# Two maxima over the partitions: from a GpSimd reduction to small matmuls and VectorE

## The chip, the cores and the metric

The kernel runs on one core of a Trainium2 chip. The metric is the device time of one execution in microseconds (us); where several executions of one kernel stand together, their median is given. Five engines work side by side, each through its own instructions in program order: PE (TensorE, matrix products; its weight loads are shown as PEld), DVE (VectorE), ACT (ScalarE), POOL (GpSimd) and SP (SyncE, which here issues every DMA).

## The reference

Input `x` has 8192 positions of 448 channels. The first half filters along the positions, the second is a gated feed-forward net. `mod` is six rows of 448, computed from a condition vector.

```python
    h = _layernorm(x, axis=-1) * (1 + ca) + sa
    x = x + ga * _A_ref(h, A_w1, A_b1, A_w2, A_b2)   # rfft, 2-layer complex block MLP, soft threshold, irfft
    h = _layernorm(x, axis=-1) * (1 + cb) + sb
    x = x + gb * _B_ref(h, B_w_gate, B_w_up, B_w_down)
    # _B_ref: (gelu(h @ w_gate) * (h @ w_up)) @ w_down, with F = 1792
```

Nothing in the reference asks for a maximum over partitions. The kernel needs two, because it carries fp32 factors as a pair of 16-bit halves and picks a power of two as the scale of each matrix: one maximum bounds the norms of the columns of `w_gate` and `w_up`, the other the rows of `w_down`.

## The kernel before, in words

There are three stages. The first (0 to 95 us) takes statistics of `x` and does the first part of the Fourier transform. The second (95 us, its first `ps`, to about 420 us) does its second part, the block MLP, the soft threshold and the first part of the inverse, and in its shadow it loads the feed-forward weights, finds their scales and splits them. The third (its matmuls on L985 run from 441.5 to 1994 us) is the last part of the inverse and the feed-forward net.

The change lies in the second stage. Its work is cut into 32 units `(h, bt)`, a half of the channels and a block of four frequencies. A loop `step(i)` works on four units at once, as a software pipeline, and the order in which it calls the parts is the order in which each engine runs them (`manual_schedule`: nothing is moved). In one step PE does, in this order:

- `stage_s2` of unit i (24 matmuls, tile `ps`); ACT and DVE split the result into `zh` and `zl`,
- `stage_m2` of unit i-2, twice (12 matmuls each, tile `pm`); DVE clips it (`t`, L427) and subtracts (`y`, four instructions on L435); `split_y` turns `y` into `yh` on ACT and `yl` on POOL,
- `stage_i1` of unit i-3, two groups of three matmuls (tile `pi`, L464 to L466); ACT copies each into `us` (L467), and SP stores `us` (`vd`, L469),
- `stage_m1` of unit i-1 (24 matmuls); ACT and DVE split it into `hh` and `hl`.

POOL's other work in a step is `tl`, the low half of the next unit's input, which PE needs for `stage_s2`.

PSUM has eight banks, used as four pairs by tag. `stage_i1` and the small products for norms take theirs from the pair `pd`. A new tile takes a bank of its pair that is free.

Side work hangs on hooks of a step, at places called `load`, `pe`, `act`, `dve`. `at(i, hook, fn)` puts `fn` there. Short DVE operations don't run at once: `later(V)` puts each into the list `tiny`, and `drip()` issues one from it. `drip()` is called eight times a step: after each `zl` (2), after each `t` and each group of `y` (4), and after each `hl` (2). So short operations stand singly between the long ones.

`row_scales` runs at step 9. At the end of step 16 `scales1` and `scales2` go into the list. They take the maximum of the norms over a partition's columns (`mx`), then over the partitions (`mxa`), and derive the scales `sw`, `dsw`, `dg`, `sa_act`, `isa`. At step 18 `down_scales` follows for `w_down` (`hs`, then `ds_d`), at step 19 `down_scales2`. The maximum over partitions is one POOL instruction, put into the same list by `GL = later(G)`. From step 18 `weights_hi` (ACT) and `weights_lo` (DVE in even steps, L709; POOL in odd ones, L711) scale and split one loaded piece `raw` per step with `sw`.

All short operations that go through `later` carry one line in the profile, L480, so they are told apart by their tiles.

Of the kernel before, what the change touches and what calls it, by code (L numbers as in the profile page):

```python
# [11 lines left out]
F32 = mybir.dt.float32  # L12
F32R = mybir.dt.float32r
F16 = mybir.dt.float16
BF16 = mybir.dt.bfloat16
I32 = mybir.dt.int32
AF = mybir.ActivationFunctionType
ALU = mybir.AluOpType

N = 8192  # L20
D = 448
# [8 lines left out]
NFT = F // 128  # L30
NP = NFT // 2
# [11 lines left out]
def spectral_geglu(ctx, tc, x, w1, b1, w2, b2, wg, wu, wd, cvec, wmod, cf1, cs2, cmi, cgm, out):  # L43
    nc = tc.nc
    V, S, G, T = nc.vector, nc.scalar, nc.gpsimd, nc.tensor
# [9 lines left out]
    cpool = ctx.enter_context(tc.tile_pool(name="cpool", bufs=1))  # L55
    psum = ctx.enter_context(tc.tile_pool(name="psum", bufs=2, space=bass.MemoryType.PSUM))

    def bank(tag, name):
        return psum.tile([128, 512], F32, tag=tag, name=name)
# [12 lines left out]
    nrm = cpool.tile([128, 2, NFT], F32, name="nrm")  # L72
# [3 lines left out]
    ds_d = cpool.tile([128, 1], F32, name="ds_d")  # L76
    sa_act = cpool.tile([128, NP], F32, name="sa_act")
    isa = cpool.tile([128, NP], F32, name="isa")
    rmax = cpool.tile([128, 2], F32, name="rmax")
# [4 lines left out]
    mpool = mctx.enter_context(tc.tile_pool(name="mpool", bufs=1, side="right"))  # L84
# [5 lines left out]
    sa0 = mpool.tile([112, NBLK], F32, name="sa0")  # L90
    mih = mpool.tile([128, 2, 128], F32R, name="mih")
    mil = mpool.tile([128, 2, 128], F32R, name="mil")

    def split(hi, lo, src, eh=None, el=None):

        (eh or S.copy)(hi, src)  # L96
        h = hi.bitcast(F32) if hi.dtype == F32R else hi
        (el or V).tensor_tensor(lo, src, h, ALU.subtract)  # L98
# [26 lines left out]
    with ExitStack() as actx:  # L125
# [136 lines left out]
        pe, start = 0.0, {}  # L262
        for g, bs in enumerate(groups):
# [5 lines left out]
            at = [pos[0] + 0.06] + [pos[i] + d for i in (1, 2, 3) for d in (0.03, 0.06)] + [pos[3] + 0.1]  # L269
            if g == 0:  # L270
                at = [t_stats[e] + 0.2] + [pos[0] + 0.03] * 7
            for t_, f in zip(at, scale_steps(bs)):
                ex(t_, f)
            for bb in bs:
                pe = start[bb] = max(pe + 0.75, at[-1] + 0.3)
# [20 lines left out]
    with ExitStack() as bctx:  # L296
# [178 lines left out]
        tiny = []  # L475
# [13 lines left out]
        VL, GL = later(V), later(G)  # L489
# [7 lines left out]
        def at(i, hook, fn, *args):  # L497
            side.setdefault((i, hook), []).append((fn, args))
# [77 lines left out]
        def inv_pow2(d, s):  # L576
            VL.tensor_scalar(d.bitcast(I32), s.bitcast(I32), -1.0, float(254 << 23), op0=ALU.mult, op1=ALU.add)
# [67 lines left out]
            ps = raws.pop(("s", pr, j))  # L645
            V.tensor_scalar(nrm[:, pr, 2 * j : 2 * j + 2], ps[:, 0:2], 1.02, 1e-30, op0=ALU.mult, op1=ALU.add)

        def all_max(dst, src):
            GL.partition_all_reduce(dst, src, 128, bass_isa.ReduceOp.max)

        mxa = cpool.tile([128, 2], F32, name="mxa")
        dsw = cpool.tile([128, 2], F32, name="dsw")
        hs = cpool.tile([128, 1], F32, name="hs")

        def scales1():

            ni = nrm.bitcast(I32)
            VL.tensor_scalar(ni, ni, 1, 0x7F800000, op0=ALU.logical_shift_right, op1=ALU.bitwise_and)
            VL.tensor_scalar(ni, ni, float(65 << 23), None, op0=ALU.add)
            mx = cpool.tile([128, 2], F32, name="mx")  # L660
            VL.tensor_reduce(mx, nrm, mybir.AxisListType.X, ALU.max)
            all_max(mxa, mx)

        def scales2():
            pow2(sw, mxa)
            inv_pow2(dsw, sw)
            inv_pow2(hs, sk)
            VL.tensor_scalar(dsw, dsw, hs, None, op0=ALU.mult)
            VL.tensor_copy(dg, dsw[:, 0:1])

            VL.tensor_tensor(hs, rmax[:, 0:1], rmax[:, 1:2], ALU.add)
            VL.tensor_tensor(hs, hs, hs, ALU.mult)
            VL.tensor_scalar(hs, hs, 1.02 * D, 1e-30, op0=ALU.mult, op1=ALU.add)
            mx2 = cpool.tile([128, NFT], F32, name="mx2")
            VL.tensor_tensor(mx2, nrm[:, 0], nrm[:, 1], ALU.mult)
            VL.tensor_scalar(mx2, mx2, hs, None, op0=ALU.mult)

            VL.tensor_tensor(sa_act, mx2[:, :NP], mx2[:, NP:], ALU.max)
            pow2(sa_act, sa_act, 13)
            inv_pow2(isa, sa_act)  # L680
            VL.tensor_scalar(sa_act, sa_act, dsw[:, 1:2], None, op0=ALU.mult)

        def down_scales():

            VL.tensor_tensor(dsc, dn[:, :NP], dn[:, NP:], ALU.max)
            VL.tensor_tensor(dsc, dsc, isa, ALU.mult)
            VL.tensor_reduce(hs, dsc, mybir.AxisListType.X, ALU.max)
            VL.tensor_scalar(hs, hs, 1e-30, None, op0=ALU.max)
            all_max(ds_d, hs)

        def down_scales2():
            pow2(hs, ds_d, 13)
# [43 lines left out]
            at(2 + 2 * j, "load", pre, npool, ("m", j), load_m, j)  # L736
            at(3 + 2 * j, "dve", down_max, j)
        at(9, "dve", row_scales)
        at(16, "dve", scales1)
        at(16, "dve", scales2)  # L740
        for i in range(1, 17):
            step(i)
        nctx.close()
# [105 lines left out]
    with ExitStack() as cctx:  # L849
# [206 lines left out]
        def down(i):  # L1056
# [59 lines left out]
        first = {  # L1116
            0: [(split_g, 1), (split_v, 1), (parts_hi, 2)],
            2: [(inverse, 1), (parts_hi, 3), (residual, 1), (parts_lo, 2, V, V)],
            3: [(sums_hi, 2), (stats2, 1)],
            4: [(rsqrt_part, 1, 5), (parts_hi, 4), (sums_lo, 2, G), (load_d8, 5), (rsqrt_part, 1, 4)],  # L1120
            5: [(parts_lo, 3, V, G), (rsqrt_part, 1, 5)],
            7: [(sums_hi, 3), (sums_lo, 3, V), (load_d8, 6)],
            8: [(norm2, 1, 0), (norm2, 1, 1), (parts_lo, 4, G, G), (parts_hi, 5)],
            10: [(pack_hi, 1), (parts_lo, 5, V, V), (pack_lo, 1), (sums_hi, 4)],
# [128 lines left out]
```

## Time and profile before

| | us |
|---|---|
| median of 3 runs | 2016.02 |
| lowest, highest | 2013.63, 2016.29 |
| the profiled execution | 2015.5 |
| its span in the profile | 2013.7 |

| busy, share of the span | PE | weight loads | DVE | ACT | POOL |
|---|---|---|---|---|---|
| whole kernel | 96% | 85% | 57% | 38% | 59% |

The span is what the profiler saw from the first to the last instruction; the profiled execution's own time is 1.8 us longer. The mean granted clock of TensorE over the span was 0.98 of full speed. A row of a timeline gives the start, the duration, the engine, the line, the operation, its tiles, and in brackets the idle time before it and what ended that. A row of the waits gives who waited for whom, the total in us, how often, and the longest. A row of a table by stretches gives for each engine its busy time, then the granted clock of TensorE, the share of the DMA engines and their rate.

### The profile page before, as it was taken

The numbers are of one execution on the slowest core, as the hardware profiler recorded it, in microseconds if no ns is written. First come the engines' busy times: TensorE is split into PE (matmuls) and PEld (weight loads), VectorE is DVE, ScalarE is ACT, GpSimd is POOL, SyncE is SP. The second block draws the span as 40 slices with busy tenths as digits, with TensorE's granted clock in tenths as the row PEclk, the third lists the DMA queues.
The fourth block names the chain that finished last, engine by engine and source line by source line (L and its number), as shares of the span: only waits on it lengthen the run. The fifth ranks groups of instructions, "written<-read, shape, count | busy, mean of one in ns | idle before, by whom it ended". The sixth has DMA issues, their size and how long they took to land.

```text
span 2013.7 us, 43598 instructions
## 1 busy us (share of the span) xinstructions
PE 1927.9 (96%) x17674; PEld 1712.5 (85%) x17674; DVE 1147.2 (57%) x2409; ACT 768.0 (38%) x1293; POOL 1197.2 (59%) x1492
## 2 busy tenths in 40 slices
PE   6799978987999999999999999999999999999999
PEld 3498968966888989898888888888888889889898
DVE  6578858868555554555555555455555555555533
ACT  3566646745233333333333333333333333333322
POOL 3444435548566666666666666666666666666644
PEclk8899988988999999999999999999999999999999
DMA  9886646741111111111111111111111111111000
GB/s 390 283 222 165 175 117 165 199 123 52 51 42 43 42 43 43 43 43 43 43 43 44 49 42 45 50 42 42 42 50 42 42 42 42 42 43 44 21 17 19
DMA packets 165569, 157.72 MB, mean 78 GB/s; under 512 B 86388, under 2 KB 146424, under 8 KB 165368
## 3 DMA queue, kind: packets, MB, share of 16 engines
q1 hardware_dynamic: 165368, 154.94, 26.6%
q8 instruction: 138, 2.26, 0.5%
q14 instruction: 63, 0.52, 0.1%
HBM read 95.09 MB, written 44.04 MB: 69 GB/s over the span
## 4 chain that ended last, share of the span: by engine, by line
PE 81%; DVE 9%; DMA 4%; ACT 2%; POOL 2%; issue 1%; SPq 1%; DVEq 0%; ACTq 0%; POOLq 0%
PE pgu L985 49%; PE pdn L1053 7%; PE pdn L1051 7%; PE pdn L1052 7%; DVE y L435 2%; DMA td<-st 2%; PE ps L183 1%; DMA raw<-in_B_w_up 1%; DVE t L427 1%; DVE zl L350 1%; DVE hl L405 1%; PE pi L885 1%; PE pi L883 1%; PE pi L884 1%; PE ps L343 1%
## 5 line engine op out<-in xcount | busy, mean ns | idle before, releaser
L985 PE MATMUL pgu<-nt,wh 128*128 128x256 f16 x6272 | 835.0, 273 | 1.2 <-DVE x L1026 1.2
L985 PEld LDWEIGHTS <-wh 128*128 128x128 f16 x6272 | 603.1, 98 | 99.3 <-issue 31.3
L985 PE MATMUL pgu<-nt,wl 128*128 128x256 f16 (+1 forms) x3584 | 502.4, 273 | 1.5 <-DVE x L1026 1.3
L1021 ACT ACTIVATE gel<-pgu,dg 128x256 f32<-128x256 f32 x448 | 200.0, 472 | 788.6 <-PE pgu L985 748.9
L1051 PE MATMUL pdn<-wd,ac 128*128 128x224 f16 x1568 | 407.8, 260 | 4.3 <-DVE x L894 2.3
L1053 PE MATMUL pdn<-wd,ac 128*128 128x224 f16 x1568 | 407.7, 260 | 0.2 <-DVE ac L1044 0.2
L1052 PE MATMUL pdn<-wd,ac 128*128 128x224 f16 x1568 | 407.7, 260 | 0.0
L1032 POOL TENSOR_TENSOR x<-x 128x128 f32<-128x128 f32 x223 | 239.9, 1076 | 234.7 <-DVE x L1026 234.7
L1044 DVE SCALAR_TENSOR_TENSOR ac<-x,sa_act,ac 128x896 f16<-128x896 f32 (+1 forms) x225 | 308.4, 1370 | 81.5 <-ACT ac L1043 81.5
L985 PEld LDWEIGHTS <-wl 128*128 128x128 f16 (+1 forms) x3584 | 298.1, 97 | 59.5 <-issue 26.1
L1026 DVE TENSOR_TENSOR x<-pgu,gel 128x256 f32<-128x256 f32 x448 | 179.6, 418 | 284.4 <-ACT gel L1021 283.7
L1043 ACT ACTIVATE ac<-x,sa_act 128x896 f16<-128x896 f32 (+1 forms) x225 | 233.0, 1035 | 53.1 <-POOL x L1035 51.2
L1086 POOL TENSOR_TENSOR o<-u,p 128x224 f32<-128x224 f32 x32 | 21.0, 656 | 292.7 <-DVE u L1085 292.7
L1033 POOL TENSOR_TENSOR x<-x 128x128 f32<-128x128 f32 x223 | 158.5, 711 | 17.5
L1052 PEld LDWEIGHTS <-ac 128*128 128x128 f16 x1568 | 154.1, 98 | 5.4 <-issue 4.7
L1051 PEld LDWEIGHTS <-ac 128*128 128x128 f16 x1568 | 154.1, 98 | 1.0 <-issue 0.2
L1053 PEld LDWEIGHTS <-ac 128*128 128x128 f16 x1568 | 154.1, 98 | 0.9 <-DVE ac L1044 0.5
L98 POOL TENSOR_TENSOR yl<-y,yh 128x448 fp32r<-128x448 f32 x63 | 74.8, 1189 | 81.1 <-ACT yh L96 81.1
L1034 POOL TENSOR_TENSOR x<-x 128x128 f32<-128x128 f32 x223 | 112.4, 504 | 0.0
L98 POOL TENSOR_TENSOR tl<-tr,th 128x896 f16<-128x896 f32 x30 | 57.7, 1924 | 89.0 <-DMA tr<-td 38.5
L1035 POOL TENSOR_TENSOR x<-x 128x128 f32<-128x128 f32 x223 | 108.1, 485 | 0.0
L435 DVE TENSOR_TENSOR y<-pm,t 64x224 f32<-64x224 f32 x256 | 99.5, 389 | 8.7 <-DVE t L427 0.5
(292 smaller groups left out, 2831.8 us busy)
## 6 DMA issues: line engine op xcount, KB each, us to landing
td<-st SPq DMA_DIRECT2D x16, 896.0 KB, 9.6
tr<-td SPq DMA_DIRECT2D x64, 224.0 KB, 4.3
vd<-us SPq DMA_DIRECT2D x64, 224.0 KB, 2.9
xx<-in_A_x SPq DMA_DIRECT2D x32, 448.0 KB, 3.4
v<-vd SPq DMA_DIRECT2D x64, 224.0 KB, 2.8
out<-x SPq DMA_DIRECT2D x31, 448.0 KB, 2.7
xt<-in_A_x SPq DMA_DIRECT2D x15, 896.0 KB, 17.2
nt<-pk SPq DMA_TRANSPOSE x480, 2.3
```

Of the source, the lines that this page charges most:

```text
L98: (el or V).tensor_tensor(lo, src, h, ALU.subtract)
L435: V.tensor_tensor(y[ri * 64 : ri * 64 + 64, gi], pv[si, ri], tv[si, ri], ALU.subtract)
L985: T.matmul(pgu[i, t, q][:, pr * H : (pr + 1) * H], w[rows, tw, f0 : f0 + 128], nts[i][rows, tn, :], start=start, stop=stop, skip_group_che ...
L1021: S.activation(gl, ps[:, :H], AF.Gelu_apprx_tanh, scale=dg)
L1026: V.tensor_tensor(dst, ps[:, H : 2 * H].rearrange("p (b c) -> p b c", b=2), gl.rearrange("p (b c) -> p b c", b=2), ALU.mult)
L1032: e.tensor_tensor(s1, a21, a22, ALU.add)
L1033: e.tensor_tensor(s2, s1, a11, ALU.subtract)
L1043: S.activation(ac[:, 0, k], x[:, k], AF.Copy, scale=sc)
L1044: V.scalar_tensor_tensor(ac[:, 1, k], x[:, k], sc, ac[:, 0, k], op0=ALU.mult, op1=ALU.subtract)
L1051: T.matmul(ps, ac[:, 0, ka], wds[t][:, 0, kb], start=t == 0, stop=False)
L1052: T.matmul(ps, ac[:, 0, ka], wds[t][:, 1, kb], start=False, stop=False)
L1053: T.matmul(ps, ac[:, 1, ka], wds[t][:, 0, kb], start=False, stop=t == NP - 1)
```

## The change

`all_max` no longer calls POOL. It rounds a column of n values per partition to bf16 (`mxc`), multiplies it with an identity on PE so that the 128 partitions come to lie along a row of PSUM (`turn`, tile `pmx`), reduces that row on DVE (`mxt`), puts the n results on a diagonal (`mxd`), and multiplies that with ones so that every partition receives them (`spread`), from where DVE copies them to the target. The values are powers of two, which bf16 holds exactly; for the second maximum an extra instruction clears the mantissa first. Between a result and its reader stand either three operations of other work, given as `first` and `then`, or three empty entries of the list. For the first maximum those six are operations that `scales2` had at a later place (`hb2`, `mx2`, `sa_act`). `scales1` and `scales2` move from the end of step 16 (`dve`) to its start (`pe`). A bf16 identity and a row of ones are made at the start of the kernel.

```diff
+    identb = mpool.tile([128, 128], BF16, name="identb")
+    make_identity(nc, identb)
+    onesr = mpool.tile([2, 128], BF16, name="onesr")
+    V.memset(onesr, 1.0)
...
-        def all_max(dst, src):
-            GL.partition_all_reduce(dst, src, 128, bass_isa.ReduceOp.max)
+        def all_max(dst, src, n, first=(), then=()):
+            col = mpool.tile([128, n], BF16, name="mxc")
+            top = mpool.tile([n, 1], F32, name="mxt")
+            dia = mpool.tile([n, n], BF16, name="mxd")
+            at_ = {}
+            free = lambda: None
+            def turn():
+                at_[0] = bank("pd", "pmx")
+                T.matmul(at_[0][:n, :128], col, identb, start=True, stop=True)
+            def spread():
+                T.matmul(at_[0][:, 128 : 128 + n], onesr[:n], dia, start=True, stop=True)
+            VL.tensor_copy(col, src)
+            tiny.extend(first or [free] * 3)
+            tiny.append(turn)
+            tiny.append(lambda: V.tensor_reduce(top, at_[0][:n, :128], mybir.AxisListType.X, ALU.max))
+            VL.tensor_scalar(dia, identb[:n, :n], top, None, op0=ALU.mult)
+            tiny.extend(then or [free] * 3)
+            tiny.append(spread)
+            tiny.append(lambda: V.tensor_copy(dst, at_[0][:, 128 : 128 + n]))
...
-            all_max(mxa, mx)
+            hb2 = cpool.tile([128, 1], F32, name="hb2")
+            mx2 = cpool.tile([128, NFT], F32, name="mx2")
+            first = [
+                lambda: V.tensor_tensor(hb2, rmax[:, 0:1], rmax[:, 1:2], ALU.add),
+                lambda: V.tensor_tensor(hb2, hb2, hb2, ALU.mult),
+                lambda: V.tensor_scalar(hb2, hb2, 1.02 * D, 1e-30, op0=ALU.mult, op1=ALU.add),
+            ]
+            then = [
+                lambda: V.tensor_tensor(mx2, nrm[:, 0], nrm[:, 1], ALU.mult),
+                lambda: V.tensor_scalar(mx2, mx2, hb2, None, op0=ALU.mult),
+                lambda: V.tensor_tensor(sa_act, mx2[:, :NP], mx2[:, NP:], ALU.max),
+            ]
+            all_max(mxa, mx, 2, first, then)
...
         def scales2():
...
-            VL.tensor_tensor(hs, rmax[:, 0:1], rmax[:, 1:2], ALU.add)
-            VL.tensor_tensor(hs, hs, hs, ALU.mult)
-            VL.tensor_scalar(hs, hs, 1.02 * D, 1e-30, op0=ALU.mult, op1=ALU.add)
-            mx2 = cpool.tile([128, NFT], F32, name="mx2")
-            VL.tensor_tensor(mx2, nrm[:, 0], nrm[:, 1], ALU.mult)
-            VL.tensor_scalar(mx2, mx2, hs, None, op0=ALU.mult)
-            VL.tensor_tensor(sa_act, mx2[:, :NP], mx2[:, NP:], ALU.max)
...
         def down_scales():
...
-            all_max(ds_d, hs)
+            VL.tensor_single_scalar(hs.bitcast(I32), hs.bitcast(I32), 0x7F800000, ALU.bitwise_and)
+            all_max(ds_d, hs, 1)
...
-        at(16, "dve", scales1)
-        at(16, "dve", scales2)
+        at(16, "pe", scales1)
+        at(16, "pe", scales2)
```

The order on POOL around the first maximum, before. `tl` and `yl` are the low halves of the input and of `y`; a row ISA without tiles is not arithmetic.

```order
L98 TENSOR_TENSOR tl<-tr,th 128x896 [waits DMAHW6_49,DMAHW7_49,PE_49,Activation_49]
L98 TENSOR_TENSOR yl<-y,yh 128x448 [waits PE_49,Activation_49] x2
L480 ISA
L480 ISA mxa<-mx 128x2 [waits DVE_49]
L98 ISA
L98 TENSOR_TENSOR tl<-tr,th 128x896 [waits DMAHW2_49,DMAHW3_49,PE_49,Activation_49]
L98 TENSOR_TENSOR yl<-y,yh 128x448 [waits PE_49,Activation_49] x2
```

And after (line numbers are three higher at this place):

```order
L101 TENSOR_TENSOR tl<-tr,th 128x896 [waits DMAHW6_49,DMAHW7_49,PE_49,Activation_49]
L101 TENSOR_TENSOR yl<-y,yh 128x448 [waits PE_49,Activation_49] x2
L101 TENSOR_TENSOR tl<-tr,th 128x896 [waits DMAHW2_49,DMAHW3_49,PE_49,Activation_49]
L101 TENSOR_TENSOR yl<-y,yh 128x448 [waits PE_49,Activation_49] x2
L101 TENSOR_TENSOR tl<-tr,th 128x896 [waits DMAHW0_49,DMAHW7_49,PE_49,Activation_49]
```

The reduction and the two ISA rows around it are gone, so `tl` follows `yl` directly; at the second maximum the same three rows go.

The order on PE at `stage_i1` of step 17, before:

```order
L419 MATMUL pm2_3400<-w2h_94,hl_3312 128x224
L464 MATMUL pi1_3423<-yh_3239,mih_98 128x448 [waits PE_49]
L465 MATMUL pi1_3423<-yl_3240,mih_98 128x448 [waits Pool_49]
L466 MATMUL pi1_3423<-yh_3239,mil_99 128x448
L464 MATMUL pi1_3428<-yh_3276,mih_98 128x448 [waits PE_49]
L465 MATMUL pi1_3428<-yl_3277,mih_98 128x448 [waits Pool_49]
L466 MATMUL pi1_3428<-yh_3276,mil_99 128x448
```

And after:

```order
L422 MATMUL pm2_3418<-w2h_94,hl_3329 128x224
L665 LDWEIGHTS onesr_105
L665 MATMUL pmx_3332<-mxd_3195,onesr_105 128x2 [waits DVE_49]
L467 MATMUL pi1_3441<-yh_3256,mih_98 128x448 [waits PE_49]
L468 MATMUL pi1_3441<-yl_3257,mih_98 128x448 [waits Pool_49]
L469 MATMUL pi1_3441<-yh_3256,mil_99 128x448
L467 MATMUL pi1_3446<-yh_3295,mih_98 128x448 [waits Activation_49]
L468 MATMUL pi1_3446<-yl_3296,mih_98 128x448 [waits Pool_49]
L469 MATMUL pi1_3446<-yh_3295,mil_99 128x448
```

The `spread` product has come in ahead of the stage, and the second group of `pi` now waits for ACT: `pmx` holds one bank of the pair `pd` from step 16 until its copy late in step 17, so both groups use the other bank, and the second needs ACT's copy of the first. Step 20 has the same.

The order on DVE in steps 16 and 17 after the change, from the first reduction to the copy of its result (`y` stands for four instructions):

```order
L483 TENSOR_REDUCE mx<-nrm 128x2
L438 TENSOR_TENSOR y<-pm_3234,t 64x224 x4
L483 CAST mxc<-mx 128x2
L430 TENSOR_SCALAR t<-pm_3260 128x448
L691 TENSOR_TENSOR hb_3191<-rmax 128x1
L438 TENSOR_TENSOR y<-pm_3260,t 64x224 x4
L692 TENSOR_TENSOR hb_3191<-hb_3191 128x1
L408 SCALAR_TENSOR_TENSOR hl<-pm_3299,hh_808 112x2x256
L693 TENSOR_SCALAR hb_3191<-hb_3191 128x1
L408 SCALAR_TENSOR_TENSOR hl<-pm_3316,hh_809 112x2x256
L353 SCALAR_TENSOR_TENSOR zl<-ps_3354,ca_96,zh_804 112x2x256
L670 TENSOR_REDUCE mxt<-pmx 2x1
```

Before, these places held no short operation until the end of step 16, and `sw<-mxa`, which waits for POOL, stood three places behind `mx`; now the list runs from step 16 to step 21.

More of the change, by code (lines that the diff above doesn't have):

```diff
@@ L6 @@
 import concourse.tile as tile
-from concourse import bass_isa
 from concourse import mybir
```

## Prediction

> **What bounds the kernel now.** I read the page first, for what ends last, then the waits of the second stage, then that stage cut into stretches of 10 us, then its timeline by engine. The page's chain of work that ended last is mostly PE's:
>
> ```profile
> PE 81%; DVE 9%; DMA 4%; ACT 2%; POOL 2%; issue 1%; SPq 1%; DVEq 0%; ACTq 0%; POOLq 0%
> ```
>
> The third stage, where nearly all of PE's share lies, is not touched. What counts is the second stage, where PE should be busy too. From the stretches (busy us of PE, PEld, DVE, ACT, POOL, then the clock granted to TensorE), an undisturbed one, and three around the two maxima:
>
> ```profile
> 240.00:250.00 10.00, 10.00 (x99) 9.76 (x98) 9.00 (x19) 5.48 (x11) 4.62 (x4) 1.00 0.49 121
> 260.00:270.00 10.00, 2.37 (x23) 2.37 (x23) 4.49 (x14) 3.67 (x7) 4.05 (x3) 0.63 0.25 68
> 300.00:310.00 10.00, 0.91 (x7) 0.71 (x7) 8.54 (x19) 2.98 (x6) 3.19 (x3) 0.51 0.17 46
> 310.00:320.00 10.00, 10.00 (x81) 9.90 (x80) 5.86 (x12) 6.58 (x10) 4.86 (x5) 0.81 0.46 115
> ```
>
> PE stands almost still twice, and after it the clock is low. Who waits for whom there (the list of waits for 235 to 440 us, and the line of the reduction itself):
>
> ```profile
> L480 POOL PARTITION_ALL_REDUCE mxa<-mx x1 | 0.4, 372 | 6.6 <-issue 6.6
> ...
> PE ps L343 <- POOL tl L98: 17.0, 2, 9.0
> DVE hs L480 <- POOL ds_d L480: 8.7, 1, 8.7
> POOL tl L98 <- issue: 7.2, 1, 7.2
> POOL ds_d L480 <- issue: 6.8, 1, 6.8
> POOL mxa L480 <- issue: 6.6, 1, 6.6
> DVE sw L480 <- POOL mxa L480: 4.3, 1, 4.3
> PE ps L341 <- DVE hs L480: 3.3, 1, 3.3
> ```
>
> The reduction takes 0.37 us, but POOL spends 6.6 and 6.8 us before the two, and 7.2 us after the first, waiting for nothing the profile shows ("issue"). The ISA rows in the order stand exactly there. DVE then sits 4.3 and 8.7 us, its queue blocked behind the reader of the result, and PE 9.0, 3.3 and 8.0 us. Then PE runs slowly:
>
> ```profile
> 267.63 0.35 PE L343 MATMUL ps<-s,tl 128*112 128x128 f16 x1 [9.00 <-POOL tl L98]
> ...
> 272.24 0.41 PE L418 MATMUL pm<-w2l,hh 112*128 112x224 f32 x1
> 272.45 0.41 PE L419 MATMUL pm<-w2h,hl 112*128 112x224 f32 x1
> ...
> 273.11 0.28 PE L417 MATMUL pm<-w2h,hh 112*128 112x224 f32 x1
> 273.23 0.27 PE L418 MATMUL pm<-w2l,hh 112*128 112x224 f32 x1
> ...
> 309.46 0.35 PE L343 MATMUL ps<-s,tl 128*112 128x128 f16 x1 [7.98 <-POOL tl L98]
> ...
> 313.85 0.28 PE L417 MATMUL pm<-w2h,hh 112*128 112x224 f32 x1
> ```
>
> Matmuls of one shape follow each other at 0.21 us until 272.9 and at 0.12 from 273.1: half speed for 5.3 us from 267.6, and for 4.4 us from 309.5 to 313.85. Half of that, 4.8 us, is lost.
>
> To size it all, the store of `us` marks one step each (step 16, step 22, and steps 23 and 28):
>
> ```profile
> 248.84 1.11 SPq L469 DMA_DIRECT2D vd<-us  x2
> ...
> 326.64 1.11 SPq L469 DMA_DIRECT2D vd<-us  x2
> ...
> 335.19 1.11 SPq L469 DMA_DIRECT2D vd<-us  x2
> ...
> 377.76 1.11 SPq L469 DMA_DIRECT2D vd<-us  x2
> ```
>
> From step 16 to 22 there are 326.64 - 248.84 = 77.8 us. Undisturbed steps take (377.76 - 335.19) / 5 = 8.51 us, with the same loads and weight splitting in them; six make 51.1. So the region costs 26.7 us more than it would without maxima and short operations. PE's waits (9.0 + 3.3 + 8.0) and the slow clock (4.8) make 25.1 of it.
>
> **The change part by part.**
>
> *The POOL reduction goes.* With it go the two idle stretches and the slow clock behind them, the whole 26.7 us, less what the new way costs in the same six steps. The cover that `tl` and `yl` need on POOL stays: undisturbed, POOL is busy 4.62 us in 10.
>
> *Four small matmuls.* Eight of one column each took 0.44 us in this chain:
>
> ```profile
> 232.82 0.44 PE pw L639 x8
> ```
>
> So 4 x 0.055 = 0.2 us, between 0 and 4 x 0.41 = 1.6 by the longest matmul shown. PE runs in order, so each could also hold all later work while it waits for its DVE operand. The operands are early: `mxc` is made in the first half of step 16's `stage_m2`, and its product stands behind six `pi` and 24 `pm` products; `mxd` is made behind the second `zl`, and its product stands behind 24 products of `stage_m2`. At 0.11 us each (273.11, 273.23) 24 products are 2.6 us. I take no wait.
>
> *The bank that `pmx` holds.* In steps 17 and 20 the second group of `pi` must wait until ACT has copied the first. The undisturbed step around 246 us shows how long:
>
> ```profile
> 245.70 1.60 DVE L435 TENSOR_TENSOR y<-pm,t 64x224 f32<-64x224 f32 x4
> 246.69 0.37 PE L464 MATMUL pi<-yh,mih 128*128 128x448 f32 x1
> 247.39 0.57 ACT L96 CAST yh<-y 128x448 fp32r<-128x448 f32 x1 [2.28 <-DVE y L435]
> 247.86 0.96 ACT L467 COPY us<-pi 128x448 f32<-128x448 f32 x2
> ```
>
> ACT's first `us` copy is queued behind `yh`, which waits for `y`. It runs from 247.86 to about 248.3 (half of 0.96), while PE wants the bank at 246.69. PE waits 1.6 us, and behind it stand `stage_m1` and so `hh` and `hl`, on which DVE waits next. Twice: 3.2 us. From below 0, if DVE is late anyway in those steps; from above 8.4, if each wait also dropped the clock (rival C).
>
> *Short operations.* The change issues 36 on DVE in these steps, against 27 before; the rest of the list are PE's or empty. What one costs depends on its place:
>
> ```profile
> 236.94 1.59 DVE L435 TENSOR_TENSOR y<-pm,t 64x224 f32<-64x224 f32 x4
> 238.57 0.62 DVE L427 TENSOR_SCALAR t<-pm 128x448 f32<-128x448 f32 x1
> ...
> 284.91 1.60 DVE L435 TENSOR_TENSOR y<-pm,t 64x224 f32<-64x224 f32 x4
> 286.54 0.17 DVE L480 TENSOR_TENSOR dsc<-dsc,isa 128x7 f32<-128x7 f32 x1
> 286.74 0.62 DVE L427 TENSOR_SCALAR t<-pm 128x448 f32<-128x448 f32 x1
> ...
> 282.32 0.16 DVE L480 TENSOR_SCALAR isa<-sa_act 128x7 int32<-128x7 int32 x1
> 282.39 0.74 DVE L350 SCALAR_TENSOR_TENSOR zl<-ps,ca,zh 112x512 fp32r<-112x512 f32 x1
> ```
>
> Between `y` and `t` it adds 1.83 - 1.63 = 0.20 us. Next to `zl` or `hl` the next one starts 0.07 later. Behind `t`, `y` has to wait for `t` anyway and it costs nothing. By the order that is 6 x 0.2 + 15 x 0.08 + 2 behind the second `y` x 0.2 = 2.8 us; between 0 (DVE has slack) and 36 x 0.2 = 7.2.
>
> *Meetings with POOL.* One short operation took far longer than its like:
>
> ```profile
> 275.96 1.15 POOL L98 TENSOR_TENSOR yl<-y,yh 128x448 fp32r<-128x448 f32 x1 [2.13 <-ACT yh L96]
> 276.00 1.14 DVE L480 TENSOR_SCALAR mx<-mx,hs 128x14 f32<-128x14 f32 x1
> ```
>
> It began 0.04 us behind a POOL operation and ended with it, against 0.16 for `isa`: 1.0 us lost. The list of 36 still holds operations of this kind (`mx2`, `sa_act` times `dsw`, `dsc` times `hs`), at other places. I keep two such meetings, 2.0 us; between 0 and one in each step, 6.
>
> *Start of the kernel.* The second identity and the ones are made before the first transform, where PE and DVE wait for the first load of `x`: nothing.
>
> The sum: 3.2 + 0.2 + 2.8 + 2.0 = 8.2 of 26.7 are given back, 18.5 us are won. The profiled execution took 2015.5 us (its span and 1.8 around it), so 1997.0; the median of the runs lies 0.5 above it, so 1997.5.
>
> **The rivals.**
>
> *A, the costs hide.* Short operations and the bank's wait fall in each other's shadow, since DVE is behind in the steps in which PE waits. For it: steps of 8.51 us end in turn on DVE and on ACT. Against: DVE is near full in these steps. Only the meetings and the matmuls remain: 2016.0 - 26.7 + 2.2 = 1991.5.
>
> *B, more meetings with POOL.* Two operations with both inputs in SBUF (`mx2`, product of two halves of `nrm`, in step 17; `dsc` times `isa` in step 19) move behind the first `t`, where POOL runs `tl`:
>
> ```profile
> 236.23 0.61 DVE L427 TENSOR_SCALAR t<-pm 128x448 f32<-128x448 f32 x1
> 236.43 1.91 POOL L98 TENSOR_TENSOR tl<-tr,th 128x896 f16<-128x896 f32 x1 [2.41 <-ACT th L96]
> ```
>
> If they are held until `tl` ends (238.34), each delays `y` by 238.34 - 236.84 = 1.5 us: 1997.5 + 3.0 = 2000.5. Against: no row of these two-input operations beside a running POOL operation exists here. [...]
>
> *C, the bank's wait drops the clock.* If each wait of PE led to half speed as the long ones did, it would cost half of 5.3 more: 1997.5 + 2 x 2.6 = 2002.7. Against: the waits are 1.6 us, the ones that did it 8 and 9.
>
> *D, slower: the new way is the longer one.* PE waits in order for `mxc` and `mxd`; with DVE late it would stand still at each of the four products, with every later matmul behind it. It decides from 18.5 / 4 = 4.6 us at each on; at 6 us each the time is 1997.5 + 24 = 2021.5. Against: 2.6 us of PE work and more stand ahead of each product whose operand DVE has just made. [...]
>
> *E, no change within 0.2%.* Another limit holds the steps up, say the loads of weights, which the idle time let run ahead. Against: the undisturbed steps have the same loads and take 8.51 us. That the change doesn't do what it says is no rival: no ISA row is left on POOL in this stage.
>
> **How the numbers follow.** The forecast has 0.61, A 0.15, B 0.13, C 0.05, D 0.03, E 0.03. Ends A and C with the runs' own scatter of about a microsecond give 1990 to 2003. A measurement of this kernel tells about 0.2% (4 us) from no change. All but D and E are faster by more than that: faster 0.94, same 0.03, slower 0.03.
>
> **What would show it.** The changed profile should have no POOL "issue" wait in this stage, no PE wait over 3 us from 240 to 320, a granted clock of 1.00 there, and 59 us (51.1 + 8.2) between the stores of steps 16 and 22. The second `pi` of steps 17 and 20 should show an idle PE of about 1.6 us, released by ACT's `us`; the four `pmx` products no wait. Stretched short operations beside `tl` would speak for B, waits at `pmx` for D. The forecast is wrong if the stores lie less than 53 or more than 65 us apart, or if the stages before and after change by more than a microsecond.

## The result: 2001.9 us, and the profile after

The changed kernel takes 2001.91 us (median of 4 runs, 2000.80 to 2002.76), the kernel before on the same chip 2015.81 us (median of 4 runs); the ratio is 0.9933, with a 95% interval of 0.9916 to 0.9950. That is 13.9 us less, where 18.5 were forecast, and inside the range. The profiled execution took 2000.8 us, its span 1999.0.

The page's chain of work that ended last is still PE's, with 1% of POOL in place of 2%:

```profile
PE 81%; DVE 9%; DMA 4%; ACT 2%; POOL 1%; SPq 1%; issue 1%; ACTq 0%; DVEq 0%; POOLq 0%
```

The stores of `us` size the stage as before (SP's timeline; steps 16, 22 and 28):

```profile
248.36 1.11 SPq L472 DMA_DIRECT2D vd<-us  x2
...
310.67 1.11 SPq L472 DMA_DIRECT2D vd<-us  x2
...
361.41 1.11 SPq L472 DMA_DIRECT2D vd<-us  x2
```

From step 16 to 22 there are now 310.67 - 248.36 = 62.3 us against 77.8, with 59.3 forecast and 51.1 undisturbed. This distance is the measure in all that follows, called the region. From the store of step 28 to the end of the span lie 1999.0 - 361.41 = 1637.6 us against 1635.9 before. In the fourteen profiles of this study it lies between 1635.9 and 1638.5, so the medians of two kernels can differ by a microsecond or two that the region doesn't show. What happens ahead of the store of step 16 it doesn't show either.

The same region by steps (a table by stretches; after the length come the busy us of PE, PEld, DVE, ACT and POOL, the granted clock, the DMA share and rate):

```profile
248.36:261.28 12.92, 9.21 (x72) 7.94 (x71) 11.68 (x26) 5.06 (x9) 4.50 (x4) 0.91 0.46 112
261.28:271.16 9.88, 9.88 (x90) 9.77 (x89) 6.83 (x20) 6.43 (x10) 3.88 (x3) 0.95 0.66 175
271.16:281.68 10.52, 10.27 (x98) 9.83 (x97) 10.24 (x24) 7.07 (x11) 4.75 (x4) 1.00 0.57 139
281.68:291.99 10.31, 8.35 (x58) 7.24 (x57) 8.97 (x22) 6.24 (x11) 6.56 (x5) 0.83 0.62 165
291.99:301.23 9.24, 9.24 (x88) 9.05 (x87) 7.26 (x15) 7.39 (x11) 3.88 (x3) 1.00 0.64 158
301.23:310.67 9.44, 8.95 (x83) 8.51 (x82) 8.06 (x18) 6.02 (x10) 6.29 (x5) 1.00 0.71 181
```

Every step is longer than the undisturbed 8.5 us, the first by 4.4. DVE is nearly full in the first (11.68 of 12.92) and third (10.24 of 10.52); the clock is low in the first two and the fourth. In the list of waits (235 to 430 us) no wait of POOL for "issue" is left, and among PE's largest in this stage are these:

```profile
PE pi L467 <- ACT us L470: 3.5, 3, 2.3
...
PE pm L417 <- ACT hh L407: 1.3, 2, 1.1
...
PE pmx L665 <- DVE mxd L483: 1.0, 1, 1.0
```

Two things in the timeline were priced too low or not at all. The first is DVE's short operations beside POOL's (timeline of both engines, six operations of the list or of `first` and `then`, each behind the POOL row that was running):

```profile
247.55 1.15 POOL L101 TENSOR_TENSOR yl<-y,yh 128x448 fp32r<-128x448 f32 x1 [1.09 <-ACT yh L99]
247.59 1.13 DVE L691 TENSOR_TENSOR hb<-rmax 128x1 f32<-128x1 f32 x1
...
253.93 1.89 POOL L101 TENSOR_TENSOR tl<-tr,th 128x896 f16<-128x896 f32 x1 [1.83 <-ACT th L99]
254.19 1.65 DVE L483 TENSOR_SCALAR mxd<-identb,mxt 2x2 bf16<-2x2 bf16 x1
256.29 0.15 DVE L697 TENSOR_TENSOR mx<-nrm 128x14 f32<-128x14 f32 x1
...
258.79 1.14 POOL L101 TENSOR_TENSOR yl<-y,yh 128x448 fp32r<-128x448 f32 x1 [2.98 <-ACT yh L99]
258.90 1.05 DVE L699 TENSOR_TENSOR sa_act<-mx 128x7 f32<-128x7 f32 x1
...
275.93 1.95 POOL L101 TENSOR_TENSOR tl<-tr,th 128x896 f16<-128x896 f32 x1 [1.31 <-ACT th L99]
276.68 1.22 DVE L483 TENSOR_TENSOR dsc<-dn 128x7 f32<-128x7 f32 x1
...
300.42 1.15 POOL L101 TENSOR_TENSOR yl<-y,yh 128x448 fp32r<-128x448 f32 x1 [1.01 <-ACT yh L99]
300.44 1.16 DVE L483 TENSOR_SCALAR dsc<-isa,hs 128x7 f32<-128x7 f32 x1
```

Five of them began while POOL's operation ran and ended with it: `mxd`, a 2 by 2 tile, took 1.65 us. Unhindered, operations like these take 0.15 to 0.22 us, as `mx` at 256.29 does. Together the five lost 5.3 us. `mx` at 256.29 is one of the two that rival B named; it went free, because DVE was late and `tl` had ended at 255.82.

The `mxd` of the second maximum, one column wide, was not held beside a running `yl`:

```profile
289.49 1.13 POOL L101 TENSOR_TENSOR yl<-y,yh 128x448 fp32r<-128x448 f32 x1 [0.98 <-ACT yh L99]
289.64 0.20 DVE L483 TENSOR_SCALAR mxd<-identb,mxt 1x1 bf16<-1x1 bf16 x1
```

The second is the clock. PE's timeline in step 17, and then in step 20:

```profile
255.89 0.16 PE L665 MATMUL pmx<-mxd,onesr 2*128 2x2 bf16 x1 [1.02 <-DVE mxd L483]
...
259.20 0.74 PE L467 MATMUL pi<-yh,mih 128*128 128x448 f32 x1 [2.34 <-ACT us L470]
...
260.49 0.41 PE L390 MATMUL pm<-zh,w1h 113*112 113x256 f32 x1
260.70 0.41 PE L391 MATMUL pm<-zl,w1h 112*112 112x256 f32 x1
...
283.88 0.37 PE L417 MATMUL pm<-w2h,hh 113*128 113x224 f32 x1 [1.09 <-ACT hh L407]
...
285.60 0.28 PE L421 MATMUL pm<-w2l,hh 112*128 112x224 f32 x1
285.71 0.27 PE L422 MATMUL pm<-w2h,hl 112*128 112x224 f32 x1
...
286.31 0.41 PE L418 MATMUL pm<-w2l,hh 113*128 113x224 f32 x1
286.53 0.41 PE L419 MATMUL pm<-w2h,hl 112*128 112x224 f32 x1
```

Products start 0.21 us apart at 260.49 and 286.31, and 0.11 apart at 285.60. The first two places are at half clock, and both follow waits far shorter than the 8 and 9 us of the kernel before. The table by stretches for the second:

```profile
283.00:286.00 3.00, 1.87 (x13) 1.57 (x13) 2.14 (x5) 3.00 (x6) 2.59 (x2) 1.00 0.87 236
286.00:289.60 3.60, 3.60 (x16) 3.29 (x15) 3.42 (x8) 1.91 (x3) 2.62 (x3) 0.53 0.99 257
```

PE was idle for 1.1 of 3 us, and then ran at half clock. The trace's record of the clock has 0.50 from 258.90 to 262.31 us and from 286.20 to 289.62, 3.41 us each. The two stretches lose 1.4 and 1.6 us of PE's time, by the spacing of their products.

### The profile page after: what moved, and what is told of

Its sections match the earlier page's. It is cut to its first block, busy times and chain, and to the rows that moved or that the text cites. A ratio compares the mean times of both kernels' runs of the same rounds, so it can differ in the third digit from the quotient of the medians.

```text
span 1999.0 us, 43611 instructions
## 1 busy us (share of the span) xinstructions
PE 1928.4 (96%) x17678; PEld 1709.9 (86%) x17678; DVE 1155.3 (58%) x2419; ACT 769.1 (38%) x1293; POOL 1198.8 (60%) x1492
## 4 chain that ended last, share of the span: by engine, by line
PE 81%; DVE 9%; DMA 4%; ACT 2%; POOL 1%; SPq 1%; issue 1%; ACTq 0%; DVEq 0%; POOLq 0%
PE pgu L1016 49%; PE pdn L1084 7%; PE pdn L1083 7%; PE pdn L1082 7%; DVE y L438 2%; DMA td<-st 2%; PE ps L186 1%; DMA raw<-in_B_w_up 1%; DVE zl L353 1%; PE pi L916 1%; DVE hl L408 1%; DVE t L430 1%; PE pi L914 1%; PE pi L915 1%; PE ps L344 0%
```

## The experiments

All were compared with the kernel before on their own chip; the table gives the region from each one's profile, and how much of it the clock record has at half clock.

| kernel | region, us | at half clock, us | median, us | ratio to before, 95% interval |
|---|---|---|---|---|
| before | 77.8 | 23.9 | 2015.8 | |
| changed | 62.3 | 6.8 | 2001.9 | 0.9933 [0.9916, 0.9950] |
| old_early | 72.1 | 17.1 | 2008.4 | 0.9968 [0.9956, 0.9981] |
| second_pool | 68.4 | 13.7 | 2008.9 | 0.9972 [0.9960, 0.9983] |
| first_pool | 68.2 | 13.7 | 2006.5 | 0.9955 [0.9941, 0.9968] |
| double_reduce | 77.2 | 23.9 | 2018.3 | 1.0010 [1.0001, 1.0019] |
| reduce_form | 58.8 | 3.4 | 1998.6 | 0.9917 [0.9905, 0.9930] |
| split_bank | 61.1 | 3.4 | 2000.9 | 0.9928 [0.9915, 0.9942] |
| both_mended | 58.8 | 6.8 | 1997.5 | 0.9910 [0.9896, 0.9923] |
| no_fillers | 61.4 | 7.5 | 2000.9 | 0.9931 [0.9919, 0.9944] |
| lean | 57.1 | 3.4 | 1997.7 | 0.9907 [0.9890, 0.9923] |
| keep_warm | 60.3 | 0 | 1999.1 | 0.9910 [0.9894, 0.9927] |
| reduce_warm | 58.9 | 3.4 | 1997.9 | 0.9911 [0.9898, 0.9925] |
| changed, again | 62.3 | 6.8 | 2002.4 | 0.9935 [0.9922, 0.9947] |

### Where the gain comes from: one maximum at a time

The changed kernel with the second maximum back on POOL:

```diff
+from concourse import bass_isa
...
-            VL.tensor_single_scalar(hs.bitcast(I32), hs.bitcast(I32), 0x7F800000, ALU.bitwise_and)
-            all_max(ds_d, hs, 1)
+            GL.partition_all_reduce(ds_d, hs, 128, bass_isa.ReduceOp.max)
```

> The changed kernel, with the second maximum back on POOL. Theory (each POOL reduction brings its own standstill): the steps 19 to 21 become long again; the stores of steps 19 and 21 lay 30.2 us apart before and 19.6 after, so about 10.6 us of the gain are lost: 2012 to 2013 us, with a POOL issue wait of about 6.8 us. Rival (the earlier start and the operations in between bring the gain, not the engine): within 1.5 us of the changed kernel, 2000.5 to 2003.5.

And with the first back on POOL:

```diff
+from concourse import bass_isa
...
-            all_max(mxa, mx, 2, first, then)
+            tiny.extend(first)
+            GL.partition_all_reduce(mxa, mx, 128, bass_isa.ReduceOp.max)
+            tiny.extend(then)
```

> The changed kernel with the first of the two maxima back on GpSimd, everything else in its place, the mirror of second_pool (2008.9 against 2001.9). Theory (each reduction on GpSimd costs a stall of its own, about half of the 13.9 us): 2006.5 to 2010, with an idle time of 6 to 8 us on GpSimd ahead of its next yl and a TensorE wait behind VectorE's y of 2 us or more. Rival (the first reduction's stall is hidden where it stands early enough, and the second made up the whole loss): 2001 to 2003.

The region grows by 6.1 us in the one case and 5.9 in the other, and the medians by 7.0 and 4.6. The theory holds for `first_pool` (2006.5 us is the low end of the forecast time) and in kind for `second_pool`, which stayed 3 us below the forecast. Each maximum on POOL is paid on its own, and the place does not hide it. POOL's timeline around the second shows the stall where it was:

```profile
288.62 0.38 POOL L484 PARTITION_ALL_REDUCE ds_d<-hs  x1 [5.72 <-DMA tr<-td]
296.24 1.12 POOL L102 TENSOR_TENSOR yl<-y,yh 128x448 fp32r<-128x448 f32 x1 [7.24 <-issue]
```

Ahead of `ds_d` the idle 5.7 us are put down to a transfer here, behind it 7.2 to nothing that the profile shows.

### What the stall belongs to: the reduction or the change of kind

The kernel before, with the first reduction issued twice in a row; nobody reads the second result:

```diff
-            all_max(mxa, mx)
+            mxd = cpool.tile([128, 2], F32, name="mxd")
+            def both():
+                for d in (mxa, mxd):
+                    G.partition_all_reduce(d, mx, 128, bass_isa.ReduceOp.max)
+            tiny.append(both)
```

> The kernel before with the first maximum over the partitions taken twice on GpSimd, the second right behind the first and read by nobody. Theory (the 6.6 us of idle time ahead of GpSimd's next operation comes when the kind of operation changes, once going to the reduction and once coming back): the second starts within 0.5 us of the first's end, the idle time ahead of the next yl is still some 6 to 8 us once, and the time is 2014 to 2018. Rival (each reduction pays for itself): a second idle time of about 6 us between the two, VectorE's y waits 6 us longer, and the time is 2020 to 2024.

POOL's timeline:

```profile
258.10 0.37 POOL L666 PARTITION_ALL_REDUCE mxa<-mx  x1 [6.92 <-issue]
258.39 0.43 POOL L666 PARTITION_ALL_REDUCE mxd<-mx  x1
265.79 1.87 POOL L98 TENSOR_TENSOR tl<-tr,th 128x896 f16<-128x896 f32 x1 [6.97 <-issue]
```

The second reduction follows without a gap; 6.9 us stand ahead of the pair and 7.0 behind it. The region is 77.2 us against 77.8. The time of 2018.3 (a ratio of 1.001) lies just above the theory's 2018 and short of the rival's 2020. So the price is one of going over to the reduction and of coming back, some 7 us each way, and the second reduction adds none; what POOL does in these 7 us the trace doesn't show.

### What the earlier place does alone

The kernel before with both maxima on POOL, but the two functions at the start of step 16:

```diff
-        at(16, "dve", scales1)
-        at(16, "dve", scales2)
+        at(16, "pe", scales1)
+        at(16, "pe", scales2)
```

> The kernel before, with the scales put at the start of step 16 as in the changed kernel, but both maxima still on POOL. Theory (the POOL reductions are the cost): no gain, 2014 to 2018 us, both standstills a little earlier. Rival (the earlier place brings the gain): 2002 to 2006.

Neither came out: 2008.4 us, a region 5.7 us shorter. The stalls are still there (8.3 us of "issue" ahead of a `yl`, DVE's `sw` 5.0 us behind `mxa`), but at the new place DVE's wait for `ds_d` is 1.0 us instead of 8.7. So with both maxima on POOL the earlier place alone gains this much; my prediction had not looked for it. No run has the new way at the old place, so how much of the change's own gain is one of place is not shown. With the place fixed, taking both maxima from POOL is worth another 72.1 - 62.3 = 9.8 us of the region, or 6.5 us of the medians.

### Meetings with POOL

The changed kernel with four of the five stretched operations in another form: three as a `tensor_reduce` with one input, `mxd` on ACT.

```diff
-            VL.tensor_scalar(dia, identb[:n, :n], top, None, op0=ALU.mult)
+            tiny.append(lambda: S.activation(dia, identb[:n, :n], AF.Copy, scale=top))
...
-                lambda: V.tensor_tensor(hb2, rmax[:, 0:1], rmax[:, 1:2], ALU.add),
+                lambda: V.tensor_reduce(hb2, rmax, mybir.AxisListType.X, ALU.add),
...
-                lambda: V.tensor_tensor(sa_act, mx2[:, :NP], mx2[:, NP:], ALU.max),
+                lambda: V.tensor_reduce(sa_act, mx2.rearrange("p (a n) -> p n a", a=2), mybir.AxisListType.X, ALU.max),
...
-            VL.tensor_tensor(dsc, dn[:, :NP], dn[:, NP:], ALU.max)
+            VL.tensor_reduce(dsc, dn.rearrange("p (a n) -> p n a", a=2), mybir.AxisListType.X, ALU.max)
```

> The changed kernel, with four short operations in another form at the same place: three two-input maxima or sums become reductions of one input (hb2, sa_act, dsc), and mxd is made on ACT. [...] Rival (they are slow for what they wait for, or DVE only meets POOL elsewhere): durations as before or other operations stretched instead, 2001 to 2003.

Expected were 0.2 to 0.3 us for each of the four, and 1997.5 to 1999.5 us in all. The kernel takes 1998.55 us, under the rival's 2001 to 2003, and its region is 3.5 us shorter. One of the two stretches of half clock went with it, so not all of the 3.5 us need be DVE's. The timeline of POOL and DVE:

```profile
247.30 1.16 POOL L101 TENSOR_TENSOR yl<-y,yh 128x448 fp32r<-128x448 f32 x1 [1.09 <-ACT yh L99]
247.34 0.14 DVE L691 TENSOR_REDUCE hb<-rmax 128x1 f32<-128x2 f32 x1
...
273.36 1.96 POOL L101 TENSOR_TENSOR tl<-tr,th 128x896 f16<-128x896 f32 x1 [1.31 <-ACT th L99]
274.12 0.15 DVE L483 TENSOR_REDUCE dsc<-dn 128x7 f32<-128x14 f32 x1
274.72 0.63 DVE L483 TENSOR_TENSOR dsc<-dsc,isa 128x7 f32<-128x7 f32 x1
```

`hb` begins 0.04 us behind POOL's `yl`, as it did in the changed kernel, and takes 0.14 instead of 1.13. The next two-input operation, `dsc` times `isa`, now falls beside `tl` and ends with it (274.72 + 0.63 = 275.35, `tl` 275.32). So in these runs it is the form of DVE's operation that decides. All fourteen profiles bear this out, for the short operations on SBUF between 230 and 330 us that began beside a POOL operation with 0.3 us or more to go. Held to its end were 24 of 24 `tensor_tensor`, 37 of 39 `tensor_scalar` with two or more columns, none of 36 `tensor_scalar` with one column, and none of 25 `tensor_reduce`. (Of the two exceptions one began 0.02 us ahead of POOL's operation, the other ran beside the reduction.) Why the form decides, the profiles don't show.

### The bank that the products hold

The changed kernel with a bank for each product, and the second product one place later:

```diff
-                T.matmul(at_[0][:, 128 : 128 + n], onesr[:n], dia, start=True, stop=True)
+                at_[1] = bank("pd", "pmy")
+                T.matmul(at_[1][:, :n], onesr[:n], dia, start=True, stop=True)
...
-            tiny.append(lambda: V.tensor_copy(dst, at_[0][:, 128 : 128 + n]))
+            tiny.append(lambda: V.tensor_copy(dst, at_[1][:, :n]))
...
-            all_max(mxa, mx, 2, first, then)
+            all_max(mxa, mx, 2, first, then + [lambda: None])
```

> The changed kernel, but the two products of a maximum take separate banks, and the second stands one place later (behind the first half of stage_m1 in step 17), so no bank is held over stage_i1. Theory (the held bank costs a PE wait of 2.3 us in step 17 and 0.6 in step 20, and the first also half a clock for 3 us): the two waits on ACT's us go, the clock stays at 1.00 in step 17, 2.5 to 4 us less, 1998 to 1999.5. Rival (DVE is behind in these steps anyway, so PE only waits elsewhere): 2001 to 2002.5.

The result lies at the rival's edge: 2000.9 us, 1.2 us less region, and the interval of the ratio overlaps the changed kernel's. PE's wait for ACT's `us` at `pi` went from 3.0 us to nothing between 235 and 330 us. But the new product `pmy` itself waited 1.6 us for that copy, a `pi` waited 1.4 us behind DVE's `mxt`, and `sw` met POOL's `tl` (1.78 us), so that ACT's weights and then `hh` came late. The wait moved. One stretch of half clock was gone here too, which may be the 1.2 us.

Both edits together:

> The changed kernel with the two edits of split_bank and reduce_form together: a bank of its own for each of the two products, the spread one place later, and the operations that a working GpSimd had stretched in a form that it did not stretch. Theory (two separate costs: the stretched operations, worth 3.4 us, and ScalarE's wait for a bank, worth 1 us): 1996.5 to 1998.5, no TensorE wait for ScalarE's us of over 1 us at the first products of a token tile. Rival (the places of the operations against the drain of the banks decide, and each edit shifts them, so that the gains do not add): 1998 to 2001, with waits of 1.4 us and more at other products.

The time of 1997.5 us, the fastest median of all, is inside the theory's range, but the region is the 58.8 us of `reduce_form` to a tenth: the gains do not add, as the rival had it. The bank's edit adds nothing that can be measured. This kernel runs 6.8 us at half clock, `reduce_form` 3.4, so what the bank is worth at an equal clock stays open.

### Operations between a result and its reader

The changed kernel without them; the six operations stand behind the first maximum:

```diff
-            tiny.extend(first or [free] * 3)
+            tiny.extend(first)
...
-            tiny.extend(then or [free] * 3)
+            tiny.extend(then)
...
-            all_max(mxa, mx, 2, first, then)
+            all_max(mxa, mx, 2)
+            late[:] = first + then
...
+            tiny.extend(late)
```

> The changed kernel without operations between a result and its reader: the three and three operations of the first maximum stand behind it, in scales2, and the second has no empty places either. Theory (one operation stands in each place between the big ones, so that 1 us or so lies between two of them anyway, while turn and spread through matmul and back take 0.3 to 0.5 us): the maximum is through after fewer places, TensorE waits at its product pmx for VectorE at most 1 us each time, and the time is 2000 to 2004. Rival (the operations between are what keeps the engines from waiting): TensorE waits at each of four products for over 1 us, with half clock behind it, 2005 to 2010.

The time of 2000.9 us is the theory's. The waits are not: PE waited over 1 us at two of the four products, and half clock followed the first of them, from 248.7 to 255.5 us (list of waits):

```profile
PE pmx L662 <- DVE mxc L483: 3.1, 2, 1.6
```

One of these waits lies in step 16, ahead of the region: the store of step 16 came 11.4 us after that of step 15, against 8.9 in the changed kernel. So the region of 61.4 us, 0.9 less than with them, flatters this kernel. From the store of step 15 to that of step 22 it took 72.8 us against 71.2. On the other side the maximum is through sooner, and four operations met POOL's for a microsecond or more instead of five. In the medians the operations in between bring nothing that can be measured here.

### The half clock

The changed kernel with 38 products between the two groups of `pi` in step 17, to fill the 2.34 us wait:

```diff
+        warm = []
...
                 S.copy(us[:, 2 * p : 2 * p + 2, :], ps[:, :D].rearrange("p (g c) -> p g c", g=2))
+                if p == 0 and warm and (h, bt) == units[14]:
+                    for _ in range(38):
+                        T.matmul(warm[0][0][:, 256:384], identb, identb, start=True, stop=True)
...
             at_ = {}
+            warm.append(at_)
```

> The changed kernel with 38 extra products of 128 x 128 whose result nobody reads, in step 17 between the two groups of pi, where TensorE stood for 2.34 us and ran at half clock for 3.3 us behind it; at 0.055 us each they fill 2.1 us of that wait. Theory (the half clock is a price of its own, set off by the short wait): no clock of 0.50 between 258 and 263 us, the second group of pi starts no later than in the changed kernel (0.1 us), the store of step 18 comes 1.2 to 1.8 us earlier against that of step 17 than before the edit (9.88 us there), and the time is 1999.5 to 2001. Rival (VectorE is behind in these steps, so that TensorE's half clock lies in its shadow): the clock stays up, but the stores of steps 17 to 22 lie as far apart as they did, and the time is 2001 to 2003.

The clock stayed at 1.00 in step 17, the region fell by 2.0 us, and the median of 1999.1 us lies just under the theory's range. The store of step 18 came 0.8 us earlier against that of step 17 (9.11 us), less than the theory's 1.2 and more than the rival's nothing; step 17 itself (12.31 against 12.92) and step 20 (9.70 against 10.31) gained 0.6 each. Step 20 gained because the second stretch was gone too, although the wait ahead of it was the same (PE's timeline, then the table by stretches):

```profile
284.54 0.37 PE L417 MATMUL pm<-w2h,hh 113*128 113x224 f32 x1 [1.09 <-ACT hh L407]
```

```profile
286.00:290.00 4.00, 2.94 (x22) 2.36 (x21) 3.82 (x9) 2.50 (x5) 3.18 (x2) 1.00 1.01 267
```

So the half clock is a price of its own, some two thirds of PE's 3.0 us visible in the region, and a wait of 1.1 us may or may not set it off. The unedited kernel once more, to see whether chance decides:

> The changed kernel once more, unedited, on another chip and on the same chip as reduce_warm. Theory (the half clock follows from the waits of TensorE alone, which the order of work fixes): 62.0 to 62.6 us between the stores of steps 16 and 22, clock of 0.50 around 259 and 287 us as before, time 2000.5 to 2003. Rival (whether a short wait lowers the clock depends on when it falls, which differs between executions): the stretches of half clock are others or fewer than two, and the stores 60 to 61.5 us apart.

The theory holds. Step 16 was stored at 250.33 us and step 22 at 312.60, which makes 62.3 again, and the two stretches began 10.51 and 37.81 us behind the store of step 16, against 10.54 and 37.84 before. With the same order of work the clock fell at the same places. It had last risen at 105.30 us in the one execution and at 107.24 in the other, 143.1 us ahead of that store in both, so from there on clock and work ran alike.

Last, `reduce_form` with 30 such products in step 17:

> The kernel of reduce_form (1998.55 us, 58.8 us between the stores of steps 16 and 22) with 30 products of 128 x 128 that nobody reads in step 17, between the two groups of pi, where TensorE stood for 1.82 us ahead of a stretch of half clock from 258.0 to 261.6 us. Theory (stretched operations and half clock are two prices, and the one stretch left costs about a microsecond): no clock of 0.50 from 246 to 312, 57.3 to 58.2 us between the stores, and 1996.5 to 1998. Rival (with the stretched operations gone the half clock lies beside VectorE's work): 58.5 to 59.2 us between the stores, 1998 to 1999.5.

The time of 1997.9 us is at the end of the theory's range, but the theory missed: the region is 58.9 us, the rival's, and no shorter than without them. The stretch in step 17 was gone, and another stood from 287.6 to 291.0 us, behind a wait of 1.79 us for ACT's `us` in step 20. The two gains do not add here; what the kernel would take with no stretch at all stays open.

### What is left

The kernel of `both_mended` with five scalings and copies on ACT instead of DVE, and two masks left out that had nothing to clear (three of the seven places):

```diff
-            pow2(sw, mxa)
+            pow2(sw, mxa, mask=False)
...
-            VL.tensor_scalar(dsw, dsw, hs, None, op0=ALU.mult)
-            VL.tensor_copy(dg, dsw[:, 0:1])
+            tiny.append(lambda: S.activation(dsw, dsw, AF.Copy, scale=hs))
+            tiny.append(lambda: S.copy(dg, dsw[:, 0:1]))
```

> The kernel of both_mended (1997.5 us) with seven short operations fewer on VectorE: five products and copies with a scale (mx2 times hb2, dsw times hs, dg, sa_act times dsw, isa times hs) go to ScalarE, and two masks of the exponent, of numbers that are powers of two already, are left out. Theory (what is left of the excess between the stores of steps 16 and 22, 58.8 us against 51.1 undisturbed, is VectorE's own time: it was busy 11.2 of the 11.5 us of step 18, and two of the operations moved were stretched there to 1.1 and 1.2 us): 56 to 57 us between the stores, and 1994.5 to 1996.5 in all. Rival (ScalarE takes the operations into the chain from y over yh and yl to the next product and pays there what VectorE saves): 58 to 60 us between the stores, 1996.5 to 1999.

The region is 57.1 us, near the theory's edge, but the median of 1997.7 is that of `both_mended`, inside the rival's range. The half clock is 3.4 us shorter than in `both_mended`, so the 1.7 us of the region can't be put down to DVE's operations alone. About 6 us over undisturbed steps remain that no run here takes away.

## Why the prediction was right, and what was mis-sized

**Right in the mechanism.** The region was to lose POOL's two stalls with DVE's and PE's waits behind them, and did: no "issue" wait of POOL, no PE wait over 3 us. `double_reduce` shows what the stall goes with, `first_pool` and `second_pool` that either one alone keeps some 6 us of the region.

**Two of its signs failed, and a third came.** The clock was not 1.00, and one of the four `pmx` products waited. The stretch behind step 28 grew by 1.7 us, where a microsecond was to speak against the forecast; the fourteen profiles spread over 2.6 us there, so this sign was drawn too narrowly.

**The sum was 3.0 us short in the region.** Forecast were 59.3 us, measured 62.3. The rest of the way from 18.5 to the profile's 14.7 us lies outside: 0.5 and 0.4 won ahead of step 16 and between 22 and 28, and 1.7 lost behind it, within the scatter of that stretch; whether part of it belongs to the change stays open. By its terms:

- *Meetings with POOL*, 2.0 us forecast, two of them: five came, 5.3 us lost. This term is mis-sized, and `reduce_form` shows it: without four of them the region is 3.5 us shorter, a stretch of half clock included. The step that failed was to count the meetings by those of the kernel before. I looked at two of the list's operations, where they would stand beside `tl` if DVE ran on time; DVE ran late, and other operations met `tl` and `yl` instead. B's direction was right, its two places were wrong, so that its 2000.5 us came within 1.4 by luck. I had also read the kernel before too narrowly. It has a second stretched `tensor_scalar` (`sa_act` times `dsw`, 1.24 us at 283.05), and the row of two SBUF inputs that I missed in weighing B stands further ahead in its timeline, in `row_scales`:

```profile
187.99 1.90 POOL L98 TENSOR_TENSOR tl<-tr,th 128x896 f16<-128x896 f32 x1 [2.64 <-ACT th L96]
188.72 1.19 DVE L480 SCALAR_TENSOR_TENSOR hb<-rmax 128x1 f32<-128x1 f32 x1
```

- *The clock*, forecast at 1.00: two stretches of half clock lost 3.0 us of PE's time, and `keep_warm` shows 2.0 of it in the region. This is rival C, which I gave 0.05 because "the waits are 1.6 us, the ones that did it 8 and 9". C had it behind the bank's wait in both steps; only the first stretch stood there, the second followed a 1.09 us wait for `hh`. The step that failed was to take the shortest wait seen to do it for the shortest that can.
- *The bank*, 3.2 us forecast in steps 17 and 20: 2.34 + 0.62 = 3.0 us of PE's idle time. The place was right, and the sum by luck, since neither wait was the 1.6 us that I took for each. But it was no loss by itself: `split_bank` took most of the wait away for 1.2 us of the region, and for nothing beside `reduce_form`.
- *Four matmuls*, no wait forecast: one waited 1.02 us, behind the stretched `mxd`. It belongs to the meetings.
- *Short operations*, 2.8 us forecast: not measured by themselves; `lean` took seven away for 1.7 us, with two stretched ones and a stretch of half clock among them.

These sizes, 5.3 + 3.0 + 3.0 + 1.0 + 2.8 + 0.2 for the products, make 15.3 us, and the excess over 51.1 is 11.2. So, if the short operations cost their 2.8, 4 us of them lie beside one another, as rival A had it in part.

**D and E.** PE did not stand at the products in order (1.0 us in all against the 4.6 each from which D decides), and the loads did not hold the steps up. **The place** I had not costed at all; `old_early` puts 5.7 us of the region on it where POOL keeps both maxima.

## What to carry to other kernels

Here a rare POOL instruction of another kind cost the way there and the way back, 7 us each, for 0.37 us of work, with DVE and PE queued behind the reader. Four small matmuls and the list's DVE operations did both maxima with 11.2 us over undisturbed steps (7.7 in `reduce_form`), where POOL at the same place left 72.1 - 51.1 = 21.0.

When short DVE operations are put between long ones beside a busy POOL, look at their form first. In these runs a reduction with one input ran through (none of 25 held), while a `tensor_tensor` on SBUF (24 of 24) or a `tensor_scalar` with more than one column (37 of 39) stood until POOL's operation ended. Price each one that can meet POOL, wherever it stands now, since a step that comes late shifts them all.

## What the runs showed of the hardware that I had not expected

TensorE's clock fell to half after short waits: 1.1 us of idle time in 3 us (step 20), 1.8 us in `reduce_form`. Each stretch lasted 3.41 us, or 6.8 us (`both_mended`, and the first of `no_fillers`). It did not follow from the length of the wait alone: the same 1.09 us wait was followed by half clock in the changed kernel and not in `keep_warm`.

In each of the fourteen profiles all recorded changes of the clock lie whole multiples of 3.413 us apart. Divided at these distances into windows of 3.413 us, the profiles from 200 to 400 us hold 767 windows at full clock. In 17 of them PE was busy, as the profile models it, for less than half of the window, and half clock followed every time. In 14 it was busy for 52 to 67%, and half clock followed six times. In 736 it was busy for 70% or more, and half clock never followed. A window in which PE was busy for 2.07 of 3.41 us was enough (step 20). The windows ahead of the two stretches of the changed kernel, and then the one with the same 1.09 us wait in `keep_warm` (tables by stretches; the first number behind the comma is PE's busy time):

```profile
255.49:258.90 3.41, 0.97 (x4) 0.48 (x3) 3.28 (x9) 0.75 (x2) 0.43 (x2) 1.00 0.06 13
282.79:286.20 3.41, 2.07 (x14) 1.71 (x15) 2.41 (x6) 3.41 (x7) 2.79 (x2) 1.00 0.90 241
```

```profile
281.90:285.32 3.42, 2.08 (x29) 1.76 (x27) 2.35 (x8) 2.31 (x5) 2.02 (x3) 1.00 0.52 136
```

Both windows with the 1.09 us wait were busy for 61%, and only that of the changed kernel was followed by half clock. What decides between 52 and 67% is not shown.

A 2 by 2 operation on DVE stood 1.65 us behind POOL, and a `tensor_tensor` of one column 1.13 us: it needs very little to be held. But a `tensor_scalar` of one column was never held (none of 36).
